# One causal mask matmul for all query tiles of a pair, three-term bounds for six pairs only, and another written-out order

## The chip, the cores and the metric

The kernel runs on one core of a Trainium2 chip. The metric is device time in microseconds (us), from many executions; lower is better. Five engines work beside each other and wait for each other by semaphores: TensorE (PE, with its weight loads shown apart as PEld), VectorE (DVE), ScalarE (ACT), GpSimd (POOL) and SyncE (SP), which issues all DMA transfers here.

## The reference

The inputs are q, k and v of shape (4, 8, 768, 64), that is 4 batches of 8 heads with 768 positions, and the weights of a gated MLP. For each query, the 24 chunks of 32 keys are ranked by an upper bound of the score, future chunks are ruled out, and ordinary attention runs over the six best chunks:

```python
k_min, k_max = k_chunks.min(axis=3), k_chunks.max(axis=3)
ub = sum(max(q * k_min, q * k_max), axis=-1)
ub = where(pos // 32 >= chunk_number, ub, -1e9)
top_chunks = argsort(ub)[..., -6:]
scores = where(chunk of key in top_chunks and key <= query, q @ k.T / 8, -1e9)
x = softmax(scores) @ v            # heads side by side: (4, 768, 512)
h = relu(x @ w_in); u, v = h[..., :512], h[..., 512:]
v_n = (v - mean(v)) / sqrt(var(v) + 1e-6)
out = (u * (w_spatial @ v_n + b_spatial)) @ w_out
```

## The kernel before, in words

Two heads make a *pair*; there are 16 pairs, 0 to 15, four to a batch. The 768 queries of a pair are six tiles of 128. Pairs 0 to 3 are worked in two halves of three tiles each (a and b), the others whole. For each pair the kernel loads q, k, v, casts them to 16 bits, turns q and k so that the head dimension lies on partitions (with PE for pairs 0 to 9, L555, and by a DMA transpose for the others), takes the maximum and the negated minimum of each key chunk (L587), and computes the bounds. From the bounds it takes the eight largest per query (L646), marks the chunks below the sixth (L669 to L674), turns the marks (PE, L692, or a DMA transpose for pairs 10 to 15), and adds them as a penalty inside the score matmuls (L736, L749, or L771 for pairs 10 to 15). ACT takes exponentials (L785), POOL zeroes the triangle above the diagonal (L796), PE multiplies with v (L819), DVE divides by the sums (L825, L830), and the result is turned (L840 by DMA, L851 by PE) for the MLP. The MLP of a batch runs when its four pairs are done: two projections (L868), statistics on DVE (L886 to L898), the spatial product (L924), the gate (L928), a turn of the result (DMA L945 or PE L937), and the output product (L953) with its store (L958).

The **bounds** of a tile can be written in two ways. With relu(q) and relu(-q), the sum of max(q·min, q·max) is relu(q)·max + relu(-q)·(-min): two matmuls per tile, and two ReLUs per pair (L601 on ACT, L603 and L605 on DVE). In the three-term form it is q·max + relu(-q)·max + relu(-q)·(-min): three matmuls per tile, and one ReLU only. The set `UB3` names the pairs of the three-term form. **Future chunks** have to be pushed below all others, but only in the four columns of each head that lie on the tile's own diagonal. For the pairs of `UB3` a matmul per tile does it (L622, `tri` times `first`, 128 x 8 columns), accumulated on the bounds; for the others one DVE addition per pair (operation `ubm`, L631).

What runs where and when is **written out by hand** in the table `ORDER`: each word is an operation, its engine (P, D, A, G for POOL, S) and the buffer slots that it takes. A function replays the table; each engine then works through its own words in that order, and waits where an operand or a buffer isn't free. The figures that each operation carries for its cost steer nothing in the replay. `ub7P:0` is the bounds of pair 7 on PE; `w0` to `w3` are fill matmuls on zeros at the start (L447), `rq0`, `rq1` the two ReLUs, `max`, `sel` and `tsel` the selection, `sc`, `exp`, `tri`, `av` the attention, `xx` the DMA transpose of its result, `ld_` the loads.

Of the kernel before, what the change touches and what calls it, by code (L numbers as in the profile page):

```python
# [151 lines left out]
UB3 = range(10)  # L152
WIDE = range(10, 16)
K_T = ()

ORDER = """
ld_k0aS:0 ld_q0aS:1 zeroD:0 preset_sna0D: identG:0 preset_vt0G: lowG:0 preset_km4G: preset_qs1G: c_k0aD:0 preset_km2D:
preset_km1G: c_q0aD:1 firstD:0 ones24D:0 ex24D:0 ld_k1aS:2 ld_q1aS:3 ld_k2aS:4 ld_k3aS:5 ld_k0bS:6 ld_q0bS:7 ld_q2aS:8
w1P:0 w3P:1 t_k0aP:0 t_q0aP:1 w2P:0 e_k0aA:0 kmm0_0aD:0 kmm1_0aD: e_q0aA: rq1_0aD:0 triG:0 km1_0aG:4 km0_0aA: ub0aP:2
max0aD:0 expandA:0 c_k1aG:2 sel0aD:0 grd0aA: t_k1aP:3 e_k1aD:1 c_k2aA:3 c_q1aG:0 preset_snb1G: tsel0aP:0 t_q1aP:1  # L160
t_k2aP:2 e_q1aA: e_k2aA:2 es0aD:0 preset_km0D: kmm1_1aD:1 kmm0_1aD: kmm0_2aD:2 c_q2aD:1 c_k3aG:2 preset_sna1G:
c_k0bG:0 rq1_1aA:1 c_q0bA:3 km0_1aG:1 km1_1aG: sc0a_0P:10 t_k0bP:3 e_k0bD: ld_q3aS:0 ld_q1bS:1 ld_k4S:0 ld_q2bS:2
ld_q3bS:3 ld_wv2S:1 ld_k2bS:4 ld_k1bS:5 ld_q7S:2 exp0a_01A:0 t_k3aP:0 t_q0bP:1 ub1aP:2 t_q2aP:3 kmm0_0bD:0 kmm1_2aD:
kmm1_0bD: max1aD:1 preset_km3D: e_k3aA:3 kmm1_3aD:1 sel1aD:0 e_q2aA: preset_snb0D: exp0a_00A: c_q2bA:0 km0_2aA:2
preset_vt3G: grd1aG: c_q1bG:2 c_q3aD:3 km1_2aG: epsG:0 km1_0bA: rq1_2aA:0 e_q0bA: kmm0_3aD: w0P:0 tsel1aP:0 es1aD:1
t_q3aP:3 ub2aP:2 t_q1bP:1 c_k1bG:1 km1_3aA:0 km0_0bG: e_q1bA: km0_3aG: max2aD:0 grd2aA:1 c_k2bA:3 c_k4G:2 sc1a_0P:10
exp1a_00A:1 exp1a_01A: e_q3aD: sel2aD: rq1_0bD:1 rq1_3aD:0 tsel2aP:0 es2aD:2 t_q2bP:1 e_q2bD: ub3aP:3 t_k4P:2 ld_q4S:3
ld_v1aS:6 ld_k3bS:7 ld_wu1S:4 ld_v2aS:8 ld_v3aS:2 ld_v0aS:1 ld_wv1S:5 ld_wu3S:6 ld_k5S:7 rq1_1bD:0 max3aD:1 sel3aD:0
grd3aD: t_k2bP:0 e_k2bA: kmm0_2bD:2 preset_vt2D: t_k1bP:1 kmm1_2bD: e_k4A:4 e_k1bA: kmm0_1bD:0 c_q7G:0 c_v1aG:0
c_q3bG:2 km1_2bG: preset_sn1G: sc2a_0P:10 av1aP:0 tsel3aP:3 rec1aD:0 es3aD:3 ub0bP:2 max0bD:0 kmm1_1bD: sel0bD:1  # L170
nrm1aD:0 t_q7P:1 t_q3bP:3 preset_vt4G: e_q3bD: c_k3bG:3 exp2a_00A:2 exp2a_01A: e_q7A:5 rq1_2bA:1 km1_1bA: c_v2aG:3
grd0bG: c_v3aG:2 c_q4G:1 km0_2bG: km0_1bA: c_wv2G:0 sc3a_0P:10 t_k3bP:1 tsel0bP:2 av2aP:0 e_k3bD: es0bD:4 ub1bP:3
t_q4P:1 tx1aP:2 rec2aD:1 max1bD:1 nrm2aD:1 sel1bD:0 ex1aD:0 exp3a_01A:3 exp3a_00A: sc0b_0P:01 c_v0aG:4 av0aP:0
rec0aD:2 nrm0aD:0 ub2bP:3 max2bD:0 kmm1_3bD:1 c_wu3G:0 av3aP:2 rec3aD:0 tx2aP:0 kmm0_3bD: nrm3aD:1 sel2bD:1 grd1bG:
c_wv1G: c_wu1G: c_k5G:0 ld_ws1S:0 ld_wv3S:2 c_ws1G:2 ld_ws3S:3 c_wv3G: ld_wv0S:1 rq1_3bA:0 e_q4A: exp0b_01A:4
exp0b_00A: tx0aP:1 sc0b_1P:10 ex0aA: ex2aD: grd2bA: exp0b_11A:5 exp0b_10A: tws1P:1 tsel1bP:2 es1bD:0 tx3aP:3 km1_3bG:
t_k5P:0 e_k5A:0 ex3aA: tsel2bP:2 ews1D:0 kmm1_4D:0 kmm1_5D:2 ld_wu2S:6 ld_k6S:5 km0_3bG: c_ws3G:3 c_wv0G: c_k6G:1
tri0b_10G: tri0b_00G: ld_q6S:4 c_q6G:2 sc1b_0P:01 tws3P:1 v0_1P:0 v0_0P:3 exp1b_01A:6 exp1b_00A: ews3D: c_wu2D:
rv0_1D:0 es2bD:1 kmm0_4D: kmm0_5D: rv0_0A:1 rq1_4D:1 sc1b_1P:10 exp1b_10A:1 exp1b_11A: ld_q5S:7 c_q5G:0 km0_4G:3
cmaskG:0 ld_ws2S:0 ld_wu0S:2 c_wu0G: c_ws2G:3 v0_2P:1 t_k6P:0 t_q5P:2 ub3bP:3 rv0_2A:2 e_k6A:1 e_q5D: bn0_2D:0  # L180
ld_v3bS:0 ld_v0bS:5 km1_4G: tri1b_10G: km1_5G:4 ld_v2bS:4 max3bD:1 sel3bD:0 grd3bD: sc2b_0P:10 u0_1P:1 t_q6P:2 ub4P:0
tsel3bP:3 exp2b_00A:2 exp2b_01A: sc2b_1P:10 ru0_1A:0 es3bA:2 bn0_0D:1 ag0_0D:0 rq1_5D:0 exp2b_11A:0 exp2b_10A: max4D:0
sel4D:1 bn0_1D:2 ld_q9S:3 ld_v1bS:6 ld_ws5S:1 ld_v4S:5 ld_wo1S:6 ld_k7S:4 ld_ws0S:7 ld_q10S:2 ld_q8S:0 u0_2P:1 c_v0bG:
av0bP:3 tws2P:0 sc3b_0P:01 ru0_2D:1 rq1_7A:1 ews2A: exp3b_01A:3 exp3b_00A: grd4G: c_q9G:1 c_v2bG: tri2b_10G:
# [24 lines left out]
km0_11G: tri8_20G: tri8_00G: c_v8G:0 es9D:3 kmm0_12D:0 sel10D: rq1_11D: o0_5P:2 eo0_4D:1 xx7S: sc9_0P:10 ub11P:3
v1_1P:1 v1_5P:0 exp9_01A:5 exp9_00A: sc9_1P:01 ld_q14S:0 ld_k14S:6 ubm11D: max11D:1 rv1_1D:0 bn1_1D:1 rv1_5A:2  # L210
rq0_12D: v1_2P:1 v1_3P:0 exp9_10A:0 exp9_11A: xs10S:5 kmm1_12D: kw1_10D: sel11D: grd11D: bn1_5D:2 so0_3S: ld_q13S:4
ld_v15S:7 ag1_5D:2 rv1_2D:1 rv1_3A:5 bn1_3D:0 sc9_2P:01 av8_0P:3 c_q14A:1 exp9_21A:2 exp9_20A: c_s12G:1 v1_4P:0
rec8_0D:2 eo0_5A:2 rv1_4A:4 bn1_2D:2 ag1_1D:3 tri9_20G: kw0_11G: km1_12G:2 c_q13G:0 v1_0P:1 rv1_0D:3 c_k14D: ag1_3D:
bn1_4D:1 bn1_0D:0 ag1_4D: ag1_0D: sc10_0P:10 u1_4P:2 av8_1P:0 u1_2P:1 nrm8_0D:0 ag1_2D: exp10_00A:6 exp10_01A:
# [55 lines left out]
def kernel(  # L270
# [171 lines left out]
    for j, n in enumerate(WARM):  # L442
        waste = buf("sc")

        def go(e, n=n, waste=waste):
            for _ in range(n):
                e.matmul(waste.t[:, 0:BANK], lhsT=zero[:, 0:P], rhs=zero, start=True, stop=True)  # L447
        op(f"w{j}", {"PE": 1.6 * t_pe(*[BANK] * n)}, go, reads=[(w_out, 0)], writes=[waste])
# [574 lines left out]
```

## Time and profile before

| | |
|---|---|
| median of three runs | 199.39 us (198.85 to 200.66) |
| the profiled execution | 198.94 us |
| its span, first to last instruction | 197.2 us |
| PE busy | 187.9 us (95%), 2252 matmuls |
| DVE busy | 165.3 us (84%) |
| ACT busy | 147.7 us (75%) |
| POOL busy | 88.5 us (45%) |
| granted TensorE clock | 0.997 |

The span is what the profile shows of one execution; the time also holds what lies around it, 1.74 us here. A busy PE counts the latency of each matmul, so its busy time is more than its work: the spacing from one start to the next is what a matmul costs when others follow it. A row of a group gives line, engine, operation, output and inputs with their sizes, the number of instructions, their busy time and mean duration in ns, and the idle time ahead of them with what ended it. A row of the timeline gives start and duration in us and the idle time ahead in brackets.

### The profile page before, as it was taken

How to read it: one execution, taken by the hardware profiler on the slowest of the kernel's cores; microseconds unless marked ns; L12 is line 12 of the kernel's file. 1: busy time of each engine (PE TensorE's matmuls, PEld its weight loads, DVE VectorE, ACT ScalarE, POOL GpSimd, SP SyncE). 2: the span in 40 equal slices, each digit the busy share in tenths (PEclk: the TensorE clock that was granted, in tenths of full speed). 3: DMA queues.
4: the chain of work that ended last, by engine and by line, in shares of the span. 5: the costliest groups of instructions: out<-in, count | busy, mean ns of one | idle time of the engine just before them, and what ended most of it. 6: DMA issues, size and time to landing. Idle time of an engine off the chain costs nothing.

```text
span 197.2 us, 5897 instructions
## 1 busy us (share of the span) xinstructions
PE 187.9 (95%) x2252; PEld 109.6 (56%) x2252; DVE 165.3 (84%) x518; ACT 147.7 (75%) x235; POOL 88.5 (45%) x169
## 2 busy tenths in 40 slices
PE   7799989999999899999999999999999999999992
PEld 2357664677655356474446666554757566444450
DVE  3799999999899999999899999979893746895350
ACT  2699999999999958868897978977997464445132
POOL 5536988688678416924346357013452420000000
PEclk9999999999999999999999999999999999999998
DMA  5999899999994999998999989899614098802445
GB/s 156 314 363 296 285 356 314 234 297 360 286 220 113 245 254 230 104 293 173 188 261 234 186 185 242 172 170 256 161 57 80 0 168 263 123 12 106 121 156 202
DMA packets 96396, 40.62 MB, mean 206 GB/s; under 512 B 83824, under 2 KB 90992, under 8 KB 96368
## 3 DMA queue, kind: packets, MB, share of 16 engines
q1 hardware_dynamic: 96368, 40.25, 84.9%
q8 instruction: 17, 0.28, 0.6%
q14 instruction: 11, 0.09, 0.1%
HBM read 24.38 MB, written 6.29 MB: 156 GB/s over the span
## 4 chain that ended last, share of the span: by engine, by line
PE 66%; DVE 18%; DMA 9%; POOL 3%; issue 2%; ACT 1%; SPq 0%; POOLq 0%; DVEq 0%; ACTq 0%
PE gen L924 15%; PE gen L868 14%; PE gen L953 11%; PE gen L819 7%; PE sc L771 7%; DVE kmm L587 5%; DMA st<-in_moe_w_spatial_dram 3%; DMA st<-in_k_dram 3%; PE sc L736 3%; DMA st<-in_v_dram 3%; PE gen L618 2%; DVE stats L886 2%; PE sc L447 2%; PE sc L749 2%; POOL n L310 2%
## 5 line engine op out<-in xcount | busy, mean ns | idle before, releaser
L785 ACT ACTIVATE e<-sc 128x768 f16<-128x768 f32 (+1 forms) x96 | 83.1, 915 | 13.6 <-PE sc L771 6.8
L796 POOL TENSOR_SCALAR_AFFINE_SELECT e<-e 128x512 f16<-128x512 f16 (+1 forms) x44 | 27.8, 643 | 43.0 <-ACT e L785 30.4
L924 PE MATMUL gen<-vn,wsT 128*128 128x512 f16 x144 | 34.0, 379 | 0.1
L587 DVE TENSOR_REDUCE kmm<-kqT 128x24 f16<-128x768 f16 (+1 forms) x40 | 30.4, 776 | 0.8 <-ACT kqT L308 0.6
L819 PEld LDWEIGHTS <-e 128*128 128x128 f16 x672 | 23.5, 97 | 4.7 <-issue 0.6
L819 PE MATMUL gen<-vt,e 128*128 128x65 f16 x672 | 25.0, 192 | 0.0
L928 DVE SCALAR_TENSOR_TENSOR late<-gen,bcol,u 128x512 f16<-128x512 f32 x24 | 17.5, 741 | 7.9 <-PE gen L924 5.2
L953 PE MATMUL gen<-w_out,late 128*128 128x512 f16 x96 | 23.5, 379 | 0.0
L924 PEld LDWEIGHTS <-wsT 128*128 128x128 f16 x144 | 13.7, 98 | 15.3 <-issue 0.6
L886 DVE BATCH_NORM_STATS2 stats<-vraw 128x6 f32<-128x512 f32 x24 | 16.1, 679 | 2.0 <-ACT vraw L875 1.8
L736 PE MATMUL sc<-kqT 64*128 64x128 f16 (+2 forms) x212 | 17.0, 271 | 0.1
L771 PE MATMUL sc<-kqT,early 128*128 128x256 f16 (+2 forms) x132 | 16.7, 267 | 0.0
L308 ACT ACTIVATE late<-gen 128x512 f32<-128x512 f32 x18 | 10.6, 598 | 6.6 <-PE gen L953 6.1
L308 ACT ACTIVATE kqT<-gen 128x384 f16<-128x384 f16 (+1 forms) x20 | 12.5, 656 | 3.8 <-PE gen L555 3.8
L875 ACT ACTIVATE u<-gen 128x512 f16<-128x512 f32 x14 | 8.4, 600 | 8.5 <-PE gen L868 8.4
L646 DVE MAX8 max<-gen 128x8 f32<-128x20 f32 (+4 forms) x160 | 14.7, 162 | 0.0
L310 POOL CAST n<-st 128x768 f16<-128x768 f32 x16 | 13.3, 831 | 2.7 <-DMA st<-in_moe_w_spatial_dram 1.4
L868 PEld LDWEIGHTS <-early 128*128 128x128 f16 x96 | 8.9, 98 | 9.8 <-issue 0.7
L953 PEld LDWEIGHTS <-late 128*128 128x128 f16 x96 | 8.8, 98 | 9.6 <-issue 0.6
L771 PEld LDWEIGHTS <-early 128*128 128x128 f16 x132 | 11.0, 98 | 5.1 <-issue 0.2
L868 PEld LDWEIGHTS <-xT 128*128 128x128 f16 x96 | 8.5, 97 | 9.7 <-issue 2.2
L868 PE MATMUL gen<-w_u,xT 128*128 128x512 f16 x48 | 12.2, 380 | 0.8 <-DVE u L877 0.8
(124 smaller groups left out, 353.6 us busy)
## 6 DMA issues: line engine op xcount, KB each, us to landing
out_dram<-late SPq DMA_DIRECT2D x24, 256.0 KB, 2.4
st<-in_k_dram SPq DMA_DIRECT2D x12, 384.0 KB, 4.7
st<-in_q_dram SPq DMA_DIRECT2D x12, 384.0 KB, 5.2
st<-in_v_dram SPq DMA_DIRECT2D x12, 384.0 KB, 4.7
st<-in_moe_w_spatial_dram SPq DMA_DIRECT2D x6, 384.0 KB, 6.0
st<-in_moe_w_in_dram SPq DMA_DIRECT2D x8, 256.0 KB, 5.4
early<-in_k_dram SPq DMA_DIRECT2D x8, 192.0 KB, 4.1
early<-in_q_dram SPq DMA_DIRECT2D x8, 192.0 KB, 4.2
```

The lines of the kernel that those rows point to most:

```text
L308: e.activation(out=out, in_=in_, func=Act.Copy)
L587: lambda e, m=m, f=f, x=x, w=w: e.tensor_reduce(kmm.t[:, m, 0:nch], x().rearrange("d (c j) -> d c j", j=w), axis=AX.X, op=f, negate=(m == 1)),
L736: e.matmul(sc[z].t[:, a:a + len(qs) * P].rearrange("p (t c) -> p t c", c=P), lhsT=kq.t[r, 0, t * P:(t + 1) * P], rhs=qv[r, qs[0]:qs[-1] + ...
L771: e.matmul(sc[z].t[:, a:a + len(qs) * P].rearrange("p (t c) -> p t c", c=P), lhsT=st["kw"].t[:, hi, t // 2, t % 2 * P:(t % 2 + 1) * P], rh ...
L785: e.activation(out=e_.t[:, z, :, 0:w], in_=x.t.rearrange("p (h c) -> p h c", h=2)[:, :, 0:w], func=Act.Exp, scale=scale)
L796: e.affine_select(out=d, in_=d, compare_op=Alu.is_ge, fill=0.0, base=0, channel_multiplier=-1, pattern=[[0, 2 * len(zs)], [1, P]])
L819: e.matmul(avv()[:, n, hi, :], lhsT=es[g].t[:, zz, hi, c:c + P], rhs=vt.t[:, t, hi, 0:D + 1], start=(t == 0), stop=(t == qi))
L868: e.matmul(acc.t, lhsT=x.t[:, ko, t * P:(t + 1) * P], rhs=w.t[:, ko, :], start=(ko == 0), stop=(ko == NDO - 1))
L886: op(f"bn{b}_{t}", {"DVE": t_dve(DH)}, lambda e, t=t, stats=stats: e.bn_stats(stats.t, vraw[t].t), reads=[vraw[t]], writes=[stats])
L924: e.matmul(acc.t, lhsT=wsT.t[:, s, t * P:(t + 1) * P], rhs=vn[s].t, start=(s == 0), stop=(s == NQT - 1))
L928: lambda e, t=t, acc=acc, g=g, a=a: e.scalar_tensor_tensor(g.t[:, a], in0=acc.t, scalar=bcol.t[:, t:t + 1], in1=u[t].t, op0=Alu.add, op1=A ...
L953: e.matmul(acc.t, lhsT=gT.t[:, a2 * KO + ko, :], rhs=w_out.t[:, ko, :], start=(ko == 0), stop=(ko == KO - 1))
```

## The change

Three things change together. `UB3` shrinks from pairs 0 to 9 to pairs 0 to 5, so pairs 6 to 9 take the two-term form and need the positive ReLU `rq0` as well. All pairs get their causal mask on PE, and by one matmul for all tiles of the pair or half: its output address walks over the diagonal blocks of the tiles, and its right side `first` is repeated for each tile. The accumulation flag that starts a bank is set by the first matmul of the first tile only. `ubm` and its DVE addition are gone for pairs 10 to 15. And the table `ORDER` is replaced by one found for a neighbouring arrangement of the work: it gives nearly every operation another place, and moves 152 operations to another engine.

```diff
-UB3 = range(10)
+UB3 = range(6)
+CAUSAL_PE = range(16)
...
-w1P:0 w3P:1 t_k0aP:0 t_q0aP:1 w2P:0 e_k0aA:0 kmm0_0aD:0 kmm1_0aD: e_q0aA: rq1_0aD:0 triG:0 km1_0aG:4 km0_0aA: ub0aP:2
...
+preset_km4G: lowG:0 ld_k1aS:2 ld_k2aS:3 ld_q3aS:4 ld_q1aS:5 ld_k0bS:6 ld_k3aS:7 ld_q0bS:8 ld_q2aS:0 w2P:0 w1P:1
+t_k0aP:0 t_q0aP:1 w3P:0 e_q0aA:0 e_k0aD: firstD:0 kmm1_0aD:0 kmm0_0aD: rq1_0aA:0 km0_0aA:4 preset_km1D: km1_0aG:
...
-        ub, causal = buf("gen"), half is not None or i in UB3
+        ub, causal = buf("gen"), half is not None or i in CAUSAL_PE
+        def diagonal():
+            u = ub.t
+            return bass.AP(u.tensor, u.offset + CPT * tiles[0], [list(u.ap[0]), [W + CPT, j], [NCH, 2], [1, CPT]])
...
-                             start=(n == 0), stop=(n == len(terms) - 1 and not causal))
-                if causal:
-                    e.matmul(ub.t[:, z * W:(z + 1) * W].rearrange("p (s c) -> p s c", c=NCH)[:, :, CPT * t:CPT * (t + 1)],
-                             lhsT=tri.t, rhs=first.t, start=False, stop=True)
+                             start=(z == 0 and n == 0 if causal else n == 0), stop=(n == len(terms) - 1 and not causal),
+                             skip_group_check=causal)
+            if causal:
+                e.matmul(diagonal(), lhsT=tri.t, rhs=first.t.unsqueeze(1).to_broadcast([P, j, 2, CPT]),
+                         start=False, stop=True, skip_group_check=True)
```

The rest of the diff changes no instruction: a cost figure of the fill matmuls, and two branches (splitting an output product, turning a single tile of the gate) whose sets are empty or hold both tiles already.

More of the change, by code (lines that the diff above doesn't have):

```diff
@@ L151 @@
 FOLDS = 0
[L152 removed]
+UB3 = range(6)
+CAUSAL_PE = range(16)
 WIDE = range(10, 16)
 K_T = ()
+SPLIT = set()
 ORDER = """
[L157 to L160 removed]
```

217 lines of the change are left out of this document (113 added, 104 removed).

## The prediction

> **What bounds the kernel now.** I read the shares of busy time first, then busy time by stretches, then waits and single rows where the change lands.
>
> ```profile
> span 197.2 us, 5897 instructions
> PE 187.9 (95%) x2252; PEld 109.6 (56%) x2252; DVE 165.3 (84%) x518; ACT 147.7 (75%) x235; POOL 88.5 (45%) x169
> ```
>
> ```profile
> 0.00:10.00 10.00, 7.41 (x58) 3.54 (x59) 5.54 (x22) 4.87 (x10) 5.54 (x20) 1.00 0.79 236
> 10.00:67.00 57.00, 54.43 (x878) 34.98 (x877) 55.39 (x188) 54.70 (x90) 42.66 (x84) 1.00 0.98 282
> 67.00:102.00 35.00, 34.68 (x500) 18.78 (x497) 33.62 (x115) 27.18 (x38) 15.62 (x28) 1.00 1.09 216
> 102.00:186.00 84.00, 84.00 (x783) 48.90 (x782) 67.77 (x191) 57.34 (x94) 24.70 (x38) 1.00 0.74 152
> ```
>
> The columns are: stretch, its length, then PE, PEld, DVE, ACT and POOL busy, granted clock, DMA share, GB/s. From 102 us on PE is busy in all of 84.00 us, and DVE and ACT have slack: a matmul fewer there is time won. From 10 to 67 us DVE is busy 97% (55.39 of 57) and ACT 96% (54.70); there PE is paced by both, although it shows 95%. PE's busy time holds overlaps, so where PE "is busy" says little in that stretch. So the program is a first stage that three engines share to about 67 us, then a long PE stage. The time of the profiled execution is 198.94 us, 1.74 us over its span; the median of the runs is 199.39. I sum against 198.94. About 1% is what a measurement of this kernel can tell from no change (its three runs lie 0.9% apart).
>
> **The change part by part.**
>
> *Bound matmuls (L618, L622).*
>
> ```profile
> L618 PE MATMUL gen<-km,rq 128*128 128x48 f16 x168 | 8.7, 183 | 0.0
> L618 PE MATMUL gen<-km,kqT 128*128 128x48 f16 x48 | 5.7, 183 | 0.0
> L622 PE MATMUL gen<-first,tri 128*128 128x8 f16 x60 | 6.9, 166 | 0.0
> ...
> 88.61 0.47 PE L618 MATMUL gen<-km,rq 128*128 128x48 f16 x12
> 88.92 0.59 PE L953 MATMUL gen<-w_out,late 128*128 128x512 f16 x2
> ```
>
> The mean of one (183, 166 ns) is latency. What one costs PE is the spacing: twelve in 88.92 - 88.61 = 0.31 us, so 25 to 26 ns, for 48 columns; I take the same for the 8-column mask. Count: each of the eight halves of pairs 0 to 3 had 3 tiles x (3 + 1) = 12 and gets 9 + 1 = 10; pairs 4 and 5 go from 24 to 19; pairs 6 to 9 from 24 to 13 (two terms in place of three, one mask in place of six); pairs 10 to 15 from 12 to 13. Sum: -16 - 10 - 44 + 6 = -64 matmuls, 64 x 25.5 = **-1.6 us** of PE. The one mask matmul writes all diagonal blocks, 48 columns, the size of a term: I cost it as a term. Its strided address is not in the trace; bounds: 8 columns cost no less than the 25 ns step, and the worst row for such a column count is latency, 183 ns once per half or pair, 20 x 0.16 = 3.2 us if nothing overlapped; I take the spacing, since the old 8-column masks are strided too and went at it. Of the 64, 37 (0.9 us) belong to pairs 0 to 6, in the first stage, and 27 (0.7 us) come later, where they count in full.
>
> *DVE and ACT operations.*
>
> ```profile
> L631 DVE TENSOR_TENSOR gen<-gen,cmask 128x48 f32<-128x48 f32 x6 | 1.3, 209 | 0.4 <-PE gen L618 0.4
> L603 DVE TENSOR_SCALAR rq<-kqT 128x768 f16<-128x768 f16 x3 | 1.6, 540 | 0.0
> L601 ACT ACTIVATE rq<-kqT 128x768 f16<-128x768 f16 x5 | 4.1, 844 | 0.0
> ```
>
> The six mask additions (1.3 us of DVE) go; they ran from 89.8 to 146.3 us where DVE has slack, so I price them at nothing; what would show them is a later selection transpose, and those wait on queues longer than 0.2 us. The positive ReLU comes in for pairs 6, 7, 9 on DVE (3 x 0.54 = 1.6 us) and for pair 8 on ACT (0.84 us), all in or just behind the first stage, where no engine has cover. That is +1.6 us on the pacing engine against the 0.9 us that PE saves there, unless the new order takes other work off.
>
> *The order.* It does. I added, for both lists, the usual start-to-start spacing of each operation's kind in the trace (2252 matmuls, 518 DVE, 234 ACT instructions) up to named places. Ahead of pair 6's first scores: PE 59.7 before, 58.0 after; DVE 61.9 and 61.6; ACT 58.7 and 58.1. Over the whole program: PE 183.3 and 181.7, DVE 161.7 and 159.4, ACT 147.1 and 149.7, POOL 87.8 and about 91.7. So DVE's excess is paid with copies and ReLUs moved to ACT and casts moved to POOL, and the first stage is no shorter in DVE work than by 0.3 us. After pair 6's first scores PE has 123.6 us of work left before and 123.7 after: part of the PE saving returns as work left for later. What decides is when PE gets through the tightest place. DVE is most ahead of PE (its work through the producer less PE's ahead of the consumer) by 1.05 us before (last half of pair 3), by 1.48 us after (spatial matmul 3 of batch 0, at 67.5 us of PE work); from there PE has 114.2 us left. Before, at the like place (pair 7's scores, 68.2 us) it has 115.1 left. With DVE as late as in this trace the end moves by -0.9 - 0.7 = **-1.6 us**, the same as by the matmul count. So I take the count.
>
> *The start.*
>
> ```profile
> 1.26 3.60 PE L447 MATMUL sc<-w_out 128*128 128x512 f16 x8 [1.26 <-DVE w_out L404]
> 4.64 0.57 PE L555 MATMUL gen<-ident,n 128*128 128x128 f16 x6
> ...
> 7.02 0.17 PE L618 MATMUL gen<-km,kqT 128*128 128x24 f16 x1 [0.73 <-POOL km L310]
> ```
>
> Eight fill matmuls go ahead of the first transposes, spaced (4.64 - 1.26) / 8 = 0.42 us; the new list has nine (groups of 5 and 4 in place of 4 and 4). The first transpose moves from 4.64 to 5.06, and all behind it up to the first bounds at 7.02 hangs on it: **+0.4 us** on the stage that DVE paces; nothing hides it, as DVE then waits. Sum: 198.94 - 1.6 + 0.4 = 197.7 us.
>
> *Queues that the new order is moved past.* Loads stand earlier or later on SP.
>
> ```profile
> 36.94 0.50 PE L555 MATMUL gen<-ident,n 128*128 128x128 f16 x6
> 66.88 0.55 PE L736 MATMUL sc<-kqT 64*128 64x384 f16 x6
> ```
>
> These are the transpose of pair 6's q, with 31.1 us of PE work ahead of it, and pair 6's first scores, with 59.7: PE runs 5.8 us late at the one and 7.2 at the other. The load of that q now stands behind 10.9 MB in place of 8.7; at 236 GB/s for 10 us and 282 after (the stretches above) it is delivered at 10 + (10.9 - 2.4) / 0.282 = 40 us, and its transpose now has 33.5 us of PE work ahead, so is due at some 39.3 to 40. I count nothing and keep 0 to 0.8 us. The transposed attention of pairs 6 and 7 (L840, SP) has less room:
>
> ```profile
> 89.88 1.48 SPq L840 DMA_TRANSPOSE early<-x16d  x1
> ...
> 94.70 0.59 PE L868 MATMUL gen<-w_v,early 128*128 128x512 f16 x2
> ...
> early<-x16d SPq DMA_TRANSPOSE x3, 3.6
> ```
>
> Issued at 89.88, with 3.6 us typical to landing it is in by 93.5, 1.2 us before its use. Between the last product that feeds it and the use lie 6.7 us of PE work before and 5.9 after: 0.4 us of room. I count 0, keep 0 to 1.3 us.
>
> **Rivals.**
>
> *1. The saving in the first stage is hidden.* PE's 0.9 us there cost nothing because DVE and ACT pace it; only 0.7 us counts, and the late start takes 0.4: 198.94 - 0.3 = 198.6, up to 199.2 with small waits. For it: 97% and 96% above. Against: the later places where DVE leads.
>
> *2. ACT takes DVE's place and the kernel gets slower.* Through the second-group exponentials of pair 5, ACT's work stood 1.25 us below PE's ahead of it, now 1.13 us above: 2.4 us more. If ACT loses as much to waits as in this trace,
>
> ```profile
> ACT e L785 <- PE sc L771: 6.8, 10, 1.7
> ACT e L785 <- PE sc L749: 6.0, 13, 1.1
> ```
>
> pair 5's scores come 2.2 us later than now: 197.7 + 2.2 = 199.9, and 201.2 if the 1.3 us of the attention transpose comes on top. It decides once ACT is more than 1 us later at pair 5 than DVE makes PE anyway. Against: many of those waits are for PE, and a loaded ACT waits less; the expansion copy (0.83 us) now runs in ACT's idle start.
>
> *3. A DVE stall goes away.*
>
> ```profile
> L898 DVE SCALAR_TENSOR_TENSOR rstd<-mv,rstd x8: 129/154/1666, 53.9 to 176.2; 128x3 f32<-128x3 f32 x8
> 61.85 1.67 DVE L898 SCALAR_TENSOR_TENSOR rstd<-mv,rstd 128x3 f32<-128x3 f32 x1
> ...
> 61.33 0.81 POOL L310 COPY qs<-kq 128x768 f16<-128x768 f16 x1
> 62.10 0.82 POOL L310 CAST kq<-st 128x768 f16<-128x768 f32 x1
> 62.88 0.62 POOL L796 TENSOR_SCALAR_AFFINE_SELECT e<-e 128x512 f16<-128x512 f16 x1
> ```
>
> One of eight 3-element operations took 1.67 us in place of 0.15 and ended at 63.52, as POOL's unbroken run of operations did (62.88 + 0.62 = 63.50). It stands on the path of the first stage. In the new order other POOL work lies beside it. If it does not come back, 1.2 to 1.5 us of DVE are won: 196.2 to 196.5. The page "SBUF — State Buffer" of the Trainium skill (section "Who interferes with whom") has a rule for it: a VectorE operation with two inputs in SBUF is shut out entirely while GpSimd holds the pair of ports they share for an operation that reads SBUF. The row agrees with it for one of eight; by this rule more POOL work means more chances of such stalls, and POOL gets 3.9 us more. Without the rule, a repeat leaves the sum as it is, and a second such stall in the first stage would cost 1.5 us: 199.2.
>
> *4. The change does not do what it says*, with the count of matmuls off by dozens, has no chance: the built program's list has 64 matmuls fewer.
>
> **How the numbers follow.** Forecast 197.7 (own range 196.7 to 198.8, from the 0.8 of the loads and up to 1 us of the stall won): chance 0.45. Rival 1: 0.22, at 198.6 to 199.2. Rival 2 and what else a wholly new order can turn up as waits: 0.20, at 199.9 to 202. Rival 3: 0.13. Faster by over 1% means below 197.4: rival 3 and some 0.4 of the forecast, 0.32. Slower by over 1% means above 201.4: the upper part of rival 2 with more than one wait, 0.16. The rest, 0.52, is within 1%. The range from 195.9 to 200.9 leaves 0.2 out, most of it above.
>
> **What would show it.** Right: 2188 matmuls; the bounds of a pair at 13 in about 0.33 us; PE busy without gaps from about 100 us on; the first bounds near 7.4 us; DVE still the busiest from 10 to 67 us. Rival 1: PE's work done at 67 us is lower than now by what the matmuls saved. Rival 2: scores of pairs 4 to 6 waiting for ACT (L785), ACT busy over 97% there. Rival 3: no L898 row beyond 0.4 us. Wrong altogether: PE idle for microseconds between 70 and 180 us, on a DMA transpose, which the new order would then have placed too late, or a changed clock.

## The result and the profile after

The changed kernel takes **207.21 us** (median of 6 runs, 206.47 to 208.59) where the kernel before takes 198.95 us beside it (6 runs, 198.72 to 200.66): a ratio of 1.0405, with a 95% interval of 1.0357 to 1.0452. The forecast was 197.7 with a range to 200.9. It was wrong in sign, and far outside its range. Medians and ranges here hold all runs; ratios leave out the few that stood over 1.5% above the fastest run of their kernel.

The page of the changed kernel, its first lines:

```profile
span 205.5 us, 5778 instructions
PE 190.0 (92%) x2188; PEld 108.6 (53%) x2188; DVE 169.8 (83%) x507; ACT 150.2 (73%) x235; POOL 91.4 (44%) x178
```

There are 64 matmuls fewer, as counted, and yet the span is 8.3 us longer (205.5 against 197.2; the profiled execution itself took 207.17 us, 1.7 over its span). Busy time by stretch of the changed kernel comes next, with the stretches and columns of the prediction, and one more row for the ten microseconds that matter:

```profile
10.00:67.00 57.00, 51.34 (x789) 32.03 (x784) 55.08 (x187) 51.22 (x86) 42.95 (x84) 0.96 1.00 289
67.00:102.00 35.00, 35.00 (x484) 18.68 (x483) 31.75 (x101) 28.91 (x42) 20.39 (x34) 0.97 0.81 162
102.00:186.00 84.00, 81.23 (x797) 47.65 (x795) 70.01 (x190) 60.60 (x95) 24.69 (x43) 1.00 0.75 160
...
60.00:70.00 10.00, 6.47 (x45) 2.46 (x46) 9.91 (x27) 3.74 (x7) 5.60 (x8) 0.66 0.84 170
```

From 60 to 70 us PE is busy 6.47 us, at a granted clock of 0.66, and ACT only 3.74 us, while DVE shows 9.91 us. Before, every stretch to 186 us had 1.00. And behind 102 us, where PE had no idle time at all, 2.77 us of it are missing (84.00 - 81.23).

The timeline at that place, PE first, then DVE, then POOL (start, duration, and in brackets the idle time ahead with what ended it):

```profile
57.88 0.47 PE L624 MATMUL gen<-km,rq 128*128 128x48 f16 x12
58.19 0.18 PE L629 MATMUL gen<-first,tri 128*128 128x48 f16 x1
58.22 0.50 PE L481 MATMUL gen<-ident,n 128*128 128x128 f16 x6
58.55 1.03 PE L873 MATMUL gen<-w_u,xT 128*128 128x512 f16 x4
63.53 0.48 PE L697 MATMUL gen<-ident,sn 128*128 128x128 f16 x3 [3.95 <-DVE vraw L882]
...
57.29 5.62 DVE L663 TENSOR_SCALAR sn<-max 128x12 f16<-128x12 f32 x1
62.80 0.68 DVE L882 TENSOR_SCALAR vraw<-gen 128x512 f32<-128x512 f32 x1
...
56.91 0.50 POOL L312 COPY km<-kmm 64x48 f16<-64x48 f16 x2 [1.91 <-DVE kmm L589]
57.36 0.82 POOL L312 CAST n<-st 128x768 f16<-128x768 f32 x1
...
61.45 0.63 POOL L801 TENSOR_SCALAR_AFFINE_SELECT e<-e 128x512 f16<-128x512 f16 x1
62.03 0.82 POOL L312 CAST kq<-st 128x768 f16<-128x768 f32 x1
67.26 0.67 POOL L801 TENSOR_SCALAR_AFFINE_SELECT e<-e 128x512 f16<-128x512 f16 x1 [4.40 <-ACT e L790]
```

The row to look at is L663 on DVE. It is the *guard* of pair 6 (grd6), which writes one extra column beside the selection's marks, 12 elements per partition; the same operation takes 0.18 us where nothing is in its way (153.44, further down). Here it takes 5.62 us. It starts as POOL is at the head of a run of operations without a gap (56.91 to 62.03 + 0.82 = 62.85) and it ends at 57.29 + 5.62 = 62.91, 0.06 us behind POOL's last. In the old order this guard stood on POOL. Everything queued behind it on DVE waits, ACT then waits for PE, and PE stands idle for 3.95 us. By the trace's clock records PE's clock is half from 62.58, 3.0 us into that gap, to 69.41 us.

The rows of L624 and L629 also show that the change itself does what was forecast: a pair's bounds are 13 matmuls in 58.22 - 57.88 = 0.34 us.

The chain of work that ended last holds the guard, and DMA transposes, which the chain of the kernel before doesn't hold. Two of them matter (start, duration):

```profile
57.38 5.53 DVE sn L663
...
153.65 4.83 DMA kqT<-qs
...
169.43 4.75 DMA late<-late
```

PE waits for both transposes, in the timeline of the changed kernel:

```profile
158.53 0.93 PE L776 MATMUL sc<-kqT,early 128*128 128x384 f16 x6 [1.06 <-DMA kqT<-qs]
...
174.22 1.04 PE L965 MATMUL gen<-w_out,late 128*128 128x512 f16 x4 [0.95 <-DMA late<-late]
```

**Where the 8.3 us are.** I use the prediction's own measure, PE's lateness: the start of an operation less the usual spacings of all PE work ahead of it. It falls only by overlap and rises with every idle gap and every slow stretch.

| where | before | after | difference added there |
|---|---|---|---|
| transposes of pair 8's k (58.2 us before, 52.9 after) | 6.7 | 7.6 | 0.9 |
| first attention values of pair 4 (60.4 before, 69.9 after) | 7.0 | 14.7 | 6.8 |
| the products with w_u of batch 1 (103.4 before, 120.1 after) | 9.8 | 15.9 | -1.6 |
| end | 9.9 | 19.8 | 3.8 |

The sum is +9.9 us; 64 matmuls at 25.5 ns take 1.6 off, and 8.3 is left, the difference of the spans. So, besides 0.9 us ahead of 55 us, three things have to be told: some 5 us net around 60 us (6.8 less the 1.6 that come back by 120 us), 3.8 us behind that, and whether the 1.6 us of the matmuls arrive at all.

### The profile page after: what moved, and what is told of

Same layout as the page of the kernel before. It is cut to its first block, busy times and chain, and to the rows that moved or that the text cites. A ratio compares the mean times of both kernels' runs of the same rounds, so it can differ in the third digit from the quotient of the medians.

```text
span 205.5 us, 5778 instructions
## 1 busy us (share of the span) xinstructions
PE 190.0 (92%) x2188; PEld 108.6 (53%) x2188; DVE 169.8 (83%) x507; ACT 150.2 (73%) x235; POOL 91.4 (44%) x178
## 4 chain that ended last, share of the span: by engine, by line
PE 56%; DVE 26%; DMA 11%; issue 3%; ACT 3%; POOL 0%; ACTq 0%; POOLq 0%; DVEq 0%
PE gen L873 13%; PE gen L929 10%; PE gen L965 8%; PE gen L824 7%; PE sc L741 5%; DVE kmm L589 5%; DMA st<-in_moe_w_in_dram 3%; PE sc L754 3%; DMA kqT<-snab 3%; PE sc L776 3%; DVE max L651 3%; DVE sn L663 3%; DMA kqT<-qs 2%; DMA late<-late 2%; DVE kqT L312 2%
## 5 line engine op out<-in xcount | busy, mean ns | idle before, releaser
L801 POOL TENSOR_SCALAR_AFFINE_SELECT e<-e 128x512 f16<-128x512 f16 (+1 forms) x44 | 26.8, 620 | 36.5 <-ACT e L790 35.0
L824 PEld LDWEIGHTS <-e 128*128 128x128 f16 x672 | 22.9, 97 | 3.6 <-issue 1.1
L824 PE MATMUL gen<-vt,e 128*128 128x65 f16 x672 | 24.4, 192 | 0.2 <-DVE u L882 0.2
L310 ACT ACTIVATE late<-gen 128x512 f32<-128x512 f32 (+1 forms) x15 | 8.8, 596 | 13.2 <-PE gen L965 13.2
L741 PE MATMUL sc<-kqT 64*128 64x128 f16 (+2 forms) x212 | 17.7, 280 | 0.1
L312 POOL CAST n<-st 128x768 f16<-128x768 f32 x18 | 14.9, 831 | 2.5 <-DMA st<-in_q_dram 1.6
L873 PEld LDWEIGHTS <-early 128*128 128x128 f16 x96 | 9.1, 98 | 10.9 <-issue 0.6
L603 ACT ACTIVATE rq<-kqT 128x768 f16<-128x768 f16 (+1 forms) x20 | 14.6, 733 | 0.3 <-DVE kqT L312 0.2
L651 DVE MAX8 max<-gen 128x8 f32<-128x20 f32 (+4 forms) x160 | 14.7, 163 | 0.0
L873 PEld LDWEIGHTS <-xT 128*128 128x128 f16 x96 | 9.0, 101 | 10.3 <-issue 3.0
L873 PE MATMUL gen<-w_u,xT 128*128 128x512 f16 x48 | 13.9, 421 | 0.1
L880 ACT ACTIVATE u<-gen 128x512 f16<-128x512 f32 x18 | 10.4, 595 | 4.7 <-PE gen L873 4.7
```

Of the source, the lines that this page charges most:

```text
L312: e.tensor_copy(out, in_)
L651: e.max(m8.t[:, t - tiles[0], s, :], ub.t[:, a:a + CPT * (t + 1)])
L741: e.matmul(sc[z].t[:, a:a + len(qs) * P].rearrange("p (t c) -> p t c", c=P), lhsT=kq.t[r, 0, t * P:(t + 1) * P], rhs=qv[r, qs[0]:qs[-1] + ...
L801: e.affine_select(out=d, in_=d, compare_op=Alu.is_ge, fill=0.0, base=0, channel_multiplier=-1, pattern=[[0, 2 * len(zs)], [1, P]])
L824: e.matmul(avv()[:, n, hi, :], lhsT=es[g].t[:, zz, hi, c:c + P], rhs=vt.t[:, t, hi, 0:D + 1], start=(t == 0), stop=(t == qi))
L873: e.matmul(acc.t, lhsT=x.t[:, ko, t * P:(t + 1) * P], rhs=w.t[:, ko, :], start=(ko == 0), stop=(ko == NDO - 1))
```

## The experiments

Where an experiment only moves operations, its diff shows the words of the order list; the letter behind a name is its engine (D DVE, A ACT, G POOL, S SP).

### What the guard waits for

Theory A: DVE is shut out for as long as POOL's run lasts; the idle PE then loses its clock. The rival: something else in the new order holds PE there, and another operation only takes the guard's place.

**e1_guard_act**, the guard on ACT:

```diff
-bn0_5D:2 grd6D: rv0_4D:5 bn0_4D:0
+bn0_5D:2 rv0_4D:5 bn0_4D:0
...
-rv0_3A:4 e_k9A: es5D:4
+rv0_3A:4 e_k9A: grd6A: es5D:4
```

> The changed kernel with one word of the order changed: the guard of pair 6 (12 numbers per partition, 5.62 us on VectorE in the changed kernel's trace) on ScalarE, ahead of the exponentials of pair 5. Theory A (the guard was shut out of VectorE's port by GpSimd's unbroken run of operations, so PE idled 3.95 us and the clock then ran at half for 6.8 us): no long guard, no PE gap at the selection transpose of pair 6, clock 1.00 from 60 to 70 us, 207.2 - 4.0 - 3.0 = 200.2 us, 199.5 to 201. Rival B (the new order is slow by its load on VectorE and ScalarE, and the guard only shows it): another operation waits in its place, PE idle between 55 and 72 us stays above 2 us, 205 us or more.

Measured 206.26 us (4 runs; ratio 1.0353, 1.0271 to 1.0436), the time that the rival gave. The timeline of this kernel, DVE, then PE, then POOL:

```profile
60.77 4.71 DVE L913 TENSOR_SCALAR vn<-vraw,rstd 128x512 f16<-128x512 f32 x2
...
66.90 0.70 PE L824 MATMUL gen<-vt,e 128*128 128x65 f16 x18 [1.89 <-DVE selT L312]
...
64.37 0.82 POOL L801 TENSOR_SCALAR_AFFINE_SELECT e<-e 128x512 f16<-128x512 f16 x1
65.14 1.65 POOL L990 MEMSET qs<- 128x1536 f16 x1
```

The guard is gone from DVE, and the next operation of its kind is caught in its place: two scalings of vn (the normalised v of the MLP) take 4.71 us (1.29 in e4, below), the first of them alone 3.93, to 64.70. POOL's run has the same words and now goes on to 69.40 us without a gap. So this operation got in while the run went on, and POOL in turn was slowed: the mask at 64.37 took 0.82 us in place of 0.63, the memset at 65.14 1.65 in place of 1.37. That the time hardly moved speaks against the guard as such, and not yet against POOL's run.

**e3_run_cut_two** and **e4_run_cut_three** leave the guard on DVE and make POOL's run shorter. e3 moves two casts (c_q11, c_k11), e4 a third one as well (c_v4; the diff is e4's):

```diff
-tri4_00G: c_v4G:1
+tri4_00G:
...
-tri5_00G: c_q11G:1 tri4_20G: c_k11G: ld_wo3S:7
+tri5_00G: tri4_20G: c_v4G:1 ld_wo3S:7
...
-ag0_5D: tri5_10G: preset_qs1G: c_s10G:0
+ag0_5D: tri5_10G: c_q11G:1 c_k11G: preset_qs1G: c_s10G:0
```

> The changed kernel, guard of pair 6 still on VectorE; two casts (k and q of pair 11) leave GpSimd's run beside it and come 5 us later. Theory A (VectorE waits until GpSimd's run has its first break): the run ends 1.6 us earlier, the guard takes 4.0 us in place of 5.6, PE's gap shrinks from 3.95 to about 2.4 us; whether the clock still drops tells from which gap on it does: time 205.6 if it does, 202.5 if it does not. Rival B (the guard is slow for another reason, such as its strided write): it stays at 5.6 us.

> As the one before, and the cast of v of pair 4 moved behind as well, so that GpSimd has to wait for the exponentials of pair 5 (done at 59.71 us) in the middle of the run. Theory A: GpSimd breaks at 59.4 to 59.7 us, the guard takes some 2.2 us, PE's gap is below 1 us, clock 1.00, 200 to 201 us. Rival B: the guard stays at 5.6 us.

One run each: 206.4 and 206.1 us. The guard's row in e3, and in e4, where POOL has to wait for ACT in the middle of the run:

```profile
58.86 4.06 DVE L663 TENSOR_SCALAR sn<-max 128x12 f16<-128x12 f32 x1
```

```profile
58.82 2.12 DVE L663 TENSOR_SCALAR sn<-max 128x12 f16<-128x12 f32 x1
...
62.75 1.29 DVE L913 TENSOR_SCALAR vn<-vraw,rstd 128x512 f16<-128x512 f32 x2
...
66.82 1.47 DVE L663 TENSOR_SCALAR sn<-max 128x12 f16<-128x12 f32 x1
...
59.67 1.22 POOL L801 TENSOR_SCALAR_AFFINE_SELECT e<-e 128x512 f16<-128x512 f16 x2
61.31 1.23 POOL L801 TENSOR_SCALAR_AFFINE_SELECT e<-e 128x512 f16<-128x512 f16 x2 [0.42 <-ACT e L790]
...
66.87 1.37 POOL L990 MEMSET qs<- 128x1536 f16 x1
```

The guard takes 5.62, 4.06 and 2.12 us as the run is cut, and ends each time with the last operation of the run (in e4 at 60.94; POOL's masks end at 59.67 + 1.22 = 60.89). In e10 below, where the run is the changed kernel's, it takes 5.60 us. That is the mechanism for the guard, by dose and effect; e1 shows that the end of the run is not always the way out. The forecasts of the time failed all the same. In e4 the guard of pair 7 was caught by a memset of POOL (66.87 + 1.37 = 68.24; the guard ends at 68.29), and PE waited there instead (0.79 and 1.34 us). What was cut from the run stood somewhere else in the same crowded queue.

**e6_front** takes both sides away: guards off DVE, the run cut, and the memset moved:

```diff
-bn0_5D:2 grd6D: rv0_4D:5
+bn0_5D:2 grd6G: rv0_4D:5
...
-ru0_3D:5 grd7D:1 sh0_1D:
+ru0_3D:5 grd7A:1 sh0_1D:
...
-preset_kw1G: tri5_20G: c_v5G:2
+preset_kw1G: tri5_20G: preset_qs1G: c_v5G:2
```

(and the three casts as in e4)

> The changed kernel with pair 6's guard on POOL (where the kernel before had it) in place of DVE, pair 7's on ACT, the memset preset_qs1 put behind tri5_20, and three of POOL's casts (c_v4, c_q11, c_k11) moved behind masks as in the third cut. Theory A (DVE shut out while POOL's run lasts, then the idle PE loses its clock): the 4.1 us wait at pair 6's selection transpose and the 2.9 us of half clock go, PE's lateness near 70 us falls from 14.7 to 8.5 to 9.5 us: 200.8 to 202.5 us, granted clock 1.00 from 55 to 75 us; if the half clock at 9.5 to 13 us shows, 1.5 us of that is in it. Rival B (the order holds PE in this place for other reasons): 204.5 to 206.5 us, as with the runs cut alone.

Measured **202.51 us** (10 runs; ratio 1.0169, 1.0132 to 1.0207), at the upper end of what A gave. Its row from 60 to 70 us, and PE's waits behind 102 us (engine, line, what it waited for, us in total, times, longest):

```profile
60.00:70.00 10.00, 9.50 (x121) 5.09 (x120) 9.98 (x31) 9.97 (x18) 8.90 (x12) 1.00 0.74 136
```

```profile
PE sc L776 <- DMA kqT<-qs: 0.9, 1, 0.9
PE gen L965 <- DMA late<-late: 0.8, 1, 0.8
```

PE is busy 9.50 us there at full clock, in place of 6.47 us at 0.66. 4.7 us of the time are told by this. What stands out in the rest are the late transposes.

### Does the lost clock cost anything of its own?

**e10_fill_idle** keeps the stall and fills PE's idle time with 16 matmuls:

```diff
-WARM = (9, 4, 5, 4)
+WARM = (9, 4, 5, 4, 16)
...
-u0_4P:0 tsel6P:3
+u0_4P:0 w4P:0 tsel6P:3
```

> The changed kernel with 16 more fill matmuls of 512 columns (their result isn't used) in PE's queue ahead of pair 6's selection transpose, where PE stands idle for 3.95 us. The guard's stall on DVE stays. Theory G (the half clock that follows the idle time is a loss of its own, 2.9 us of PE's lateness): granted clock 1.00 from 60 to 72 us, and 207.2 - 2.9 = 204.3 us (203.8 to 205.0). Rival H (DVE, which lost 5.4 us, paces the stage to 75 us; a PE at full clock only waits for it there, so the half clock is hidden): clock 1.00 too, but 206.2 to 207.4 us.

Measured 205.77 us (4 runs, 204.14, 204.75, 206.79 and 209.41; ratio 1.0325, 1.0240 to 1.0409): two runs lie in G's range and one in H's, so the times don't choose. The trace tells more (PE's timeline, then the row of a stretch):

```profile
60.90 3.62 PE L449 MATMUL sc<-w_out 128*128 128x512 f16 x16
65.01 0.33 PE L697 MATMUL gen<-ident,sn 128*128 128x128 f16 x3 [0.49 <-DVE vraw L882]
...
60.00:75.00 15.00, 13.66 (x141) 6.95 (x139) 14.96 (x35) 10.05 (x16) 11.22 (x15) 1.00 0.62 124
```

The clock stays at 1.00 there. Pair 5's last scores ahead of the guard start 1.49 us later than in the changed kernel's profile (a different start, see below), the second spatial product (s0_1) only 0.19 us later: 1.3 us are won between the two. With the clock lost, the same matmuls take 2.7 us longer (6.40 us from 63.53 to 69.93 in the changed kernel, 3.74 from 65.01 to 68.75 here). So about half of the 2.7 us count and the rest is hidden, as PE at full clock waits for DVE, which is busy 14.96 of 15 us. Neither G nor H holds alone. From there to its end this profile wins another 2.6 us on the changed kernel's. PE's wait for pair 15's transpose is gone and the one for xg2_3 is 0.3 us in place of 0.95, without an edit there: 1.7 of the 2.6.

### The late transposes

Pair 15's scores wait for the transpose xs15, issued at 153.65 in the changed kernel, once its guard has been through DVE's queue. The kernel before issued its one at 149.15, with the scores 4.8 us behind it; now 158.53 - 1.06 - 153.65 = 3.8 us are left for it. For the other one, xg2_3, the same sum gives 174.22 - 0.95 - 169.43 = 3.8 us. The rows are of the changed kernel on DVE, and of the kernel before on SP:

```profile
151.98 1.12 DVE L913 TENSOR_SCALAR vn<-vraw,rstd 128x512 f16<-128x512 f32 x1
...
153.44 0.18 DVE L663 TENSOR_SCALAR qs<-max 128x12 f16<-128x12 f32 x1
```

```profile
149.15 1.45 SPq L681 DMA_TRANSPOSE kqT<-qs  x1
```

But too late an issue is only half of it. In e10 the same transpose has the same distance, 156.76 - 152.95 = 3.8 us, and PE doesn't wait (SP, then PE; last, from the page of the changed kernel, a DMA queue with its packets and MB):

```profile
152.95 1.64 SPq L686 DMA_TRANSPOSE kqT<-qs  x1
...
156.76 0.93 PE L776 MATMUL sc<-kqT,early 128*128 128x384 f16 x6
...
q8 instruction: 17, 0.28, 0.6%
```

It landed 3.67 us after its issue in e10 and 3.65 in the kernel before, but 4.83 in the changed kernel. The packets in the traces show what differs: queue 8, which the page calls "instruction", moves 17 blocks of 16 KB, and in the changed kernel one of them ran from 155.64 to 156.61, in the middle of the transpose; in e10 one ran from 153.01 to 154.07, as the transpose was being issued. In the profiles of all 17 kernels, xs15 landed after 3.65 to 3.88 us in the six without such a block between issue and landing, and after 4.02 to 5.34 in ten with one; e10, with its block at the issue, is the seventeenth. For xg2_3 it was 4.75 us in the changed kernel, with a block, and 2.72 to 2.80 in e5, e7 and e9, without. With the shorter landing both would have been in time in the changed kernel. So the new order left little room, and a longer landing used it up. That the block itself delays the transpose is argued from this agreement; no experiment moves a block alone.

**e5_late_transposes** moves the guard, a copy, a gating product and a transpose ahead:

```diff
-max15D:0 sel15D:1 rs2_0A: u2_1P:1
+max15D:0 sel15D:1 c_s15D: grd15D: rs2_0A: u2_1P:1
...
-vn2_0D:3 c_s15D: rec12_1D:0
+vn2_0D:3 rec12_1D:0
...
-sh2_1D: grd15D: o1_1P:1
+sh2_1D: o1_1P:1
...
-g2_3D:1 xg2_1S:0 so1_1S: so1_4S: so1_0S: xx13S:1
-o2_1P:2 g2_5D:0 eo2_1D:2 g2_2D: xg2_3S:1
+g2_3D:1 g2_2D: xg2_1S:0 xg2_3S:1 so1_1S: so1_4S: so1_0S: xx13S:1
+o2_1P:2 g2_5D:0 eo2_1D:2
```

> The changed kernel with pair 15's guard and its copy c_s15 put directly behind sel15 on DVE (so that the transpose xs15 can be issued some 2 us earlier), and with the gating product g2_2 and the transpose xg2_3 put directly behind g2_3 and xg2_1. Theory C (behind 100 us PE alone sets the end, and two transposes are issued too late): the waits of 1.06 us ahead of pair 15's first scores and of 0.95 us ahead of the output matmul o2_3 go, and both count in full: 207.2 - 1.2 - 1.1 = 204.9 us (204.4 to 205.4). Rival D (the loss is all made in the first stage, and what is won behind it is only waited for elsewhere): 206.5 to 207.3 us.

Measured 206.28 us (4 runs; ratio 1.0324, 1.0242 to 1.0405): 0.9 us won, not 2.3, and that not clear of the changed kernel's interval. **e7_front_and_late** is e5 and e6 together.

> The edits of the two other runs together. If both theories A and C hold, the gains add: 198.4 to 200.4 us, within 1% of the kernel before, and the long remainder is told. If the gains don't add (D), 200.8 us or more.

Measured 201.39 us (10 runs; ratio 1.0065, 1.0029 to 1.0101), 1 us above the forecast. Both profiles show why; the lines are of e7, PE and then DVE:

```profile
164.43 1.02 PE L965 MATMUL gen<-w_out,late 128*128 128x512 f16 x4 [1.11 <-DVE late L312]
...
163.69 0.69 DVE L312 COPY late<-gen 128x512 f32<-128x512 f32 x1 [1.71 <-DMA out_dram<-late]
```

The transposes are in time, but one of them (xg2_3) now stood ahead of three stores on SP. The copy that empties o2_1's bank waits for a store (1.71 us), and the next output matmul for the copy (1.11 us). It was my edit that made this wait. **e9_both_stores_first** puts the transpose behind the stores:

```diff
-xg2_1S:0 xg2_3S:1 so1_1S: so1_4S: so1_0S: xx13S:1
+xg2_1S:0 so1_1S: so1_4S: so1_0S: xg2_3S:1 xx13S:1
```

> The edits of e7, but with the transpose xg2_3 put behind the three stores that follow xg2_1 on SP in place of ahead of them. In e7 the wait moved to the output matmul o2_0 (1.11 us), whose bank is emptied by the copy eo2_1, and that copy waited for a store behind xg2_3. Theory C (each late wait counts in full, once nothing takes its place): 201.4 - 1.1 = 200.3 us (199.6 to 200.9), and no PE wait over 0.5 us behind 100 us. Rival D (a new wait takes its place again): 201.0 to 201.8 us.

Measured **199.91 us** (10 runs, before 199.02 beside it; ratio 1.0038, 1.0011 to 1.0065). PE's longest wait behind 102 us is now:

```profile
PE sc L776 <- DMA kqT<-snab: 0.4, 1, 0.4
```

With ten words of the order list moved or given to another engine, the changed kernel is within half a per cent of the old one, 0.9 us above it. Most of the loss is told: 4.7 us by DVE's stall and what follows it, 2.6 us (e9 against e6) by the edits to two transposes. PE's waits for them in e6's profile are 1.7 us; what the remaining 0.9 of the 2.6 is stays open.

### What the edits are worth without the order

**e2_edits_old_order**: the edits in the old order. The six mask additions (ubm10 to ubm15) go, the four ReLUs come in behind their sisters:

```diff
-ubm10D:
...
-rq1_6D:0
+rq1_6D:0 rq0_6D:
...
-rq1_7A:1
+rq1_7A:1 rq0_7D:
...
-rq1_8D:0
+rq1_8D:0 rq0_8A:
...
-rq1_9D:0
+rq1_9D:0 rq0_9D:
```

> The edits without the new order: the kernel before's order, with the six mask additions of VectorE taken out and the positive ReLU of pairs 6, 7 and 9 on VectorE and of pair 8 on ScalarE put in right behind the negative ones. 64 matmuls fewer, as in the changed kernel. Theory A (the loss is the order's alone; the edits save PE 1.6 us, of which at least the 0.7 us of the later stage arrive): 197.3 to 198.6 us. Rival B (the edits themselves cost, by the strided mask matmul or the four ReLUs): 200 us or more.

Measured 200.45 us (10 runs, before 199.4; ratio 1.0053, 1.0006 to 1.0099). 64 matmuls fewer, and nothing won, as rival B has it. **e8_mask_old_order** has the merged mask, but three terms for pairs 6 to 9 and no added ReLUs (against e2's text):

```diff
-UB3 = range(6)
+UB3 = range(10)
```

> The order of the kernel before with the merged mask alone: one mask matmul for a pair in place of three or six, the mask additions on DVE of pairs 10 to 15 gone, pairs 6 to 9 still bounded in three terms without the extra ReLUs; 40 matmuls fewer than before. Theory E (of the edits, it is the four ReLUs in the first stage that cost; what PE saves there is hidden): 198.7 to 199.5 us beside 199.4 before. Rival F (the merged, strided mask matmul itself costs time): 200.3 us or more, as with all edits in the old order (200.45).

Measured 199.02 us (10 runs, before 199.54; ratio 0.9967, 0.9928 to 1.0006). The first stage of e2, then of e8:

```profile
10.00:67.00 57.00, 53.92 (x833) 33.95 (x831) 55.92 (x188) 53.10 (x88) 40.91 (x81) 1.00 0.96 277
```

```profile
10.00:67.00 57.00, 54.41 (x847) 34.51 (x846) 55.02 (x187) 54.19 (x90) 41.88 (x84) 1.00 0.97 281
```

DVE is busy 55.92 us of 57 in e2 and 55.02 in e8, which has 24 matmuls more and is the faster by 1.7 us, going by the two ratios (their intervals just touch). In the old order the ReLUs cost more than the matmuls they save. No cost of the merged mask shows. Whether its 40 matmuls, 1.0 us, are won stays open: the interval runs from 1.4 us faster to 0.1 slower.

### The stall that the kernel before has

**e11_before_run_cut** is the kernel before with its own short stall (sh0_1, 1.67 us) taken away:

```diff
-c_q11G:1 c_v5G:0 preset_sn0G:
+preset_sn0G:
...
-tri5_20G: c_k11G: tri5_10G:
+tri5_20G: tri5_10G: c_q11G:1 c_k11G: c_v5G:0
```

> The kernel before, with POOL's casts c_q11, c_k11 and c_v5 moved behind the mask tri5_10, so that POOL's unbroken run beside sh0_1 (the 3-element operation of 1.67 us) ends some 1.5 us earlier. If rival 3 of the prediction holds (that stall stands on the path of the first stage): the operation takes 0.2 to 0.4 us, and 199.4 - 1.2 = 198.2 us (197.7 to 198.7), ratio 0.990 to 0.997. If it is covered: 199.1 to 199.7 us.

```profile
62.62 0.15 DVE L898 SCALAR_TENSOR_TENSOR rstd<-mv,rstd 128x3 f32<-128x3 f32 x1
```

The stall is gone (0.15 us) and PE's 0.77 us wait behind it too, and the time is 199.65 us (12 runs, before 199.02; ratio 1.0023, 0.9986 to 1.0059): nothing won. Ahead of the place, at pair 4's first attention values, PE's lateness is 7.8 us in this profile (7.0 before), and small waits bring it to 10.9 by 125 us (9.8 before): what was won there was given back. **e12_mask_run_cut**, the same cut in e8's kernel:

> The same cut of POOL's run in the kernel of e8 (the old order with the merged mask alone). If both gains stand: 199.0 - 1.2 = 197.8 us (197.2 to 198.4), ratio 0.988 to 0.995, faster than both kernels of the case. If the stall was covered: 198.7 to 199.3 us.

198.97 us (12 runs; ratio 0.9994, 0.9962 to 1.0026): covered as well. No kernel here beats the old one by more than its interval.

### The start

In most profiles of the new order the clock is half from about 9.5 to 13 us, in the changed kernel's own it isn't. Four more fill matmuls go into the idle time there, in the changed kernel (**e13_start_fill**) and in that of e9 (**e14_all_and_start**):

```diff
-t_k1aP:3 e_k1aA:1
+t_k1aP:3 w4P:1 e_k1aA:1
```

> The changed kernel with four more fill matmuls in PE's queue behind the transposes of pair 1's k, in the idle time ahead of the first selection transpose (0.9 us). In five of the seven profiles of the new order the granted clock is half from about 9.5 to 13 us, and all behind it is some 1.5 us later; the kernel before never shows it. Theory J (the half clock there comes from too little PE work in the stretch from 6 to 9.5 us, and it costs what it delays): granted clock 1.00 from 9 to 16 us, and 207.2 - 0.7 = 206.5 us (205.6 to 206.9), since some of the changed kernel's runs have it and some not. Rival K (other waits of the first stage take it up, as DVE paces it): 206.9 to 207.6 us with the same clock.

> The kernel of e9 (guards off DVE, POOL's run cut, late transposes mended) with the same four fill matmuls at the start. J: 199.9 - 1.0 = 198.9 us (198.3 to 199.4), ratio to the kernel before 0.995 to 1.001. K: 199.6 to 200.2 us.

206.91 us (4 runs; ratio 1.0366, 1.0307 to 1.0424) and 199.47 us (12 runs, before 199.33; ratio 1.0008, 0.9977 to 1.0038). The clock is full at the start in both. The stretch from 10 to 20 us in e9, and in e14 with a wait further on:

```profile
10.00:20.00 10.00, 9.52 (x122) 6.06 (x121) 8.71 (x35) 8.78 (x20) 5.47 (x17) 0.85 0.99 262
```

```profile
10.00:20.00 10.00, 9.34 (x136) 5.99 (x136) 9.68 (x45) 9.54 (x23) 5.93 (x19) 1.00 0.90 252
...
30.47 1.02 PE L873 MATMUL gen<-w_v,xT 128*128 128x512 f16 x4 [1.30 <-POOL w_v L312]
```

At 11 us e14 is 1.4 us ahead of e9, and at 30 us it has given all of that back, to a weight that isn't cast yet (the wait of 1.30 us; e9 has none there). So in these two profiles the half clock at the start is hidden, which speaks for K; the times alone don't separate the two.

**e15_all_start_three_terms** is e14 without the four ReLUs:

> The kernel of e14 without the four added ReLUs of pairs 6 to 9: these pairs are bounded in three terms again (24 matmuls more, 0.6 us of PE; 1.6 us less of DVE and 0.8 us less of ACT). If DVE paces the new order's first stage too (theory E): 198.9 - 1.0 = 197.9 us (197.3 to 198.6), ratio 0.990 to 0.997, faster than both kernels of the case. If not: 198.9 + 0.3 = 199.2 us (198.8 to 199.6).

200.19 us (12 runs; ratio 1.0048, 1.0017 to 1.0079). Not faster: what e2 and e8 show for the old order doesn't hold in the new one. Why it is slower stays open; its profiled execution (199.97 us, e14's 200.14) doesn't show the difference.

## Why the prediction was wrong

**Bound matmuls: right as a term.** 2188 matmuls, 13 in 0.34 us, the strided mask at the spacing. Whether the 1.6 us reach the time stays open. In the old order all the edits together bring nothing (e2), but the four ReLUs are among them; the mask alone (e8) fits its whole 1.0 us as well as none. So rival 1, "The saving in the first stage is hidden", is neither shown nor ruled out.

**DVE and ACT operations: half right.** The mask additions are worth nothing, as priced. The ReLUs cost in the old order what the prediction feared (e2 against e8), about 1.7 us, and in the new order no such cost shows (e15).

**The order: the step that failed.** "I added, for both lists, the usual start-to-start spacing of each operation's kind", then "With DVE as late as in this trace" and "So I take the count". A sum of usual durations treats every operation as if its duration went with it wherever it is put. The new order moved pair 6's guard from POOL to DVE, beside an unbroken run of POOL, where it took 5.62 us in place of 0.18. DVE did not stay as late as in the old trace, it lost 5.4 us there. No sum by engine can show that: DVE's total even came out lower. The guards are in the diff, each with its engine letter, and a list of operations that change engines would have shown it.

**Rival 3 had the mechanism, with the wrong sign and the wrong price.** It read one 1.67 us stall that ended with POOL's run and asked whether it would go away; a second one was priced at 1.5 us, the size of the first. For the guard the price was not the size of the stall seen, but the length of POOL's run left when it comes: 5.6 us, 4.1 or 2.1 as the run was cut. Even its first half failed on the chip: without that stall the kernel before is no faster (e11).

The Trainium skill's page "SBUF — State Buffer", section "Who interferes with whom", lets a tensor_scalar or a cast in a two-port mode contend with GpSimd, and blocks the later one for the whole of the other's instruction. The rows agree that DVE is shut out, by an operation with one input in SBUF, where the prediction had looked at operations with two; whether the guard ran in such a mode, they don't tell. They differ in the measure: it is not one instruction, but eight of POOL's in a row (57.36 to 62.85). L882, which reads PE's result memory and not SBUF, is never caught (654 to 693 ns in all its 19 instructions in the changed kernel). It also falls unevenly. Beside POOL's longer run from 47.6 to 55.0 us in the same profile no operation of DVE is stretched by over 0.3 us, and why one is caught and another not stays open.

**The clock** has no term in the prediction at all, only the words "or a changed clock" under what would prove it wrong. PE's idle 3.95 us went with 6.83 us at half clock, 2.40 us in e3 with 3.41 us, 1.89 us in e1 (and 0.95 soon after) with 6.83 us; behind the start, no wait of 1.54 us or less (e12) alone did. It counted for about 1.3 us (e10). The Trainium skill's page "TensorE: Matmul & The Clock Gate", section "What's actually happening", has a free-running window of about 3.4 us in which PE's activity is judged; 6.83 is two of them and 3.41 one, so the lengths agree, and that the start differs between executions of one order fits it too. How much idle time inside a window is enough, the traces only bound: 1.89 us was, 1.54 us was not.

**Queues: looked at the wrong transposes.** The prediction checked one load and the L840 transpose of pairs 6 and 7, found room and kept 0 to 0.8 and 0 to 1.3 us. It took the "3.6 us typical to landing"; by that figure xs15, with its 3.8 us, passes too. Against the longest landings of a selection transpose in the kernel before (L681: 3.6, 4.8 and 5.9 us shortest, median and longest) it is short, as it was at 4.83: "PE idle for microseconds between 70 and 180 us, on a DMA transpose, which the new order would then have placed too late" was written down as a sign, and not worked out for the other transposes. The edits to two of them won 2.6 us (e9 against e6).

**Start: too dear, and hidden.** +0.4 was counted; the first bounds came 0.18 us later in the changed kernel's profile (7.20 against 7.02), and in e14 against e9 1.4 us of a later start are taken up by 30 us.

**Rival 2 (ACT)** did not come: in e9, where the stall is gone, ACT is busy 54.98 us of 57 in the first stage, 54.70 before, and PE's only wait for it there of 0.2 us or more is one of 0.4 us, for a guard (L661). The mechanism that came had no chance of its own; it falls under "what else a wholly new order can turn up as waits", which was given up to 202 us.

## What to carry to other kernels

When an order list is made anew, don't add up engines only: list the operations that changed engine, and for each look at what runs unbroken on POOL beside it; a small DVE operation with its data in SBUF can wait there for the whole run. Check each DMA transpose by its own distance, from the end of its last input to its use, against the longest landing time that the trace shows for its kind, not the typical one. And a matmul saved in a stage that other engines pace is not time saved, until an experiment with that edit alone says so.

## What the hardware showed that was not expected

- A DVE operation of 12 elements waited 5.62 us, to the end of eight POOL operations in a row, and 1.27 to 1.47 us behind a single memset of POOL that reads nothing (e4: 66.82 to 68.29, memset 66.87 to 68.24).
- Lost clock and lost time are not the same: of 2.7 us that PE's matmuls took longer at half clock, 1.3 us counted in the stage that DVE paces.
- The same DMA transpose landed 4.83 us after its issue in the changed kernel and 3.67 in e10, with the same words around it, and PE's wait for it (1.06 us, none) came and went with that. The longer landings are those with a 16 KB block of queue 8 in their midst.
